# Another fixed order of the same 2689 steps in a chunked attention with a split-precision feed-forward layer

## The chip, the core and the metric

The kernel runs on one core of a Trainium2 chip. The metric is the device time of one execution in microseconds; less is better. The core has TensorE (PE, matmuls and transposes), VectorE (DVE), ScalarE (ACT), GpSimd (POOL) and SyncE (SP), which here issues every DMA transfer. Each engine works through its own list of instructions in order and waits for the others through semaphores.

## The reference

```python
def _attn_ref(q, k, v):                  # each (8, 8, 576, 64), float32
    q_c = q.reshape(B, H, nc, 64, D)     # chunks of 64 positions; k_c, v_c alike
    scores = scale * np.matmul(q_c, k_c.transpose(0, 1, 2, 4, 3))
    scores = scores - np.max(scores, axis=-1, keepdims=True)
    attn = np.exp(scores)
    attn = attn / (np.sum(attn, axis=-1, keepdims=True) + 1e-09)
    out = np.matmul(attn, v_c)
...
    x = attn_out.transpose(0, 2, 1, 3).reshape(B * S, H * D)   # (4608, 512)
    h = x @ w_in                          # w_in (512, 2048), float64
    g = h * (1.0 / (1.0 + np.exp(-1.702 * h)))
    return (g @ w_out).astype(np.float32) # w_out (2048, 512), float64
```

## The kernel before

The 4608 tokens are cut into 36 tiles of 128 and 9 blocks of 512. Attention makes x for a tile; the feed-forward part takes a block at a time through 16 slices of 128 hidden units. Each float32 product is made of three matmuls on a high and a low part (low x with high w, high x with high w, high x with low w), so x, g and the weights are all split in two. The first three blocks are computed plainly; the other six go in three pairs with seven instead of eight products for a 2 by 2 scheme of halves (`plan_two`), and the last pair's second matrix product too (`plan_o`).

All work is cut into steps. `plan.add(engine, cost, rank, fn, need, make, take, give)` names a step by its `make`: it needs other steps, takes buffers and gives them back. What order they are issued in is a string, `ORDER`, with the 2689 names in a row; `Plan.emit` runs through it and calls each step's function, so that every engine's list of instructions, SP's transfers among them, is the list of its steps in that order. The costs and ranks in `plan.add` decide nothing once the list is fixed. Two kinds of steps that the rows below show most:

- The first four token tiles (`plan_first`, u = 0 to 3), ahead of everything: load q and k (`q_u`, `k_u`) and v (`v_u`); transposes on PE (`tqp_u`, `tkp_u`, L453, tiles qkTp_u_0 and qkTp_u_1), copied out by ACT (`tq_u`, `tk_u`; tile 0's k by DVE); scores on PE (`s_u`, L474); row maximum and subtraction on DVE (`m_u`, `sm_u`, L480, L484); exponential on ACT (`ex_u`); sum and reciprocal on DVE (`z_u`, L491 to L494); normalisation on POOL (`n_u`, L497); transposes on PE (`ep_u`, L502), copied by ACT (`et_u`, L509); x on PE (`xp_u`, L518); x's high part on ACT (`xh_u`, L526), its low part on DVE (`xl_u`, L529). `xp_u` takes both buffers of the tag `att`, and `xl_u` gives them back, so one tile's x is read out before the next is made.
- The weights' 16 blocks (`plan_w`, j = 0 to 15): two loads of 512 KB of float64 words (`raw_j`, L335 and L339), scaling on ACT (`wsc_j`, L343), low words on ACT (`wlow_j`, L347), a shift on DVE (`wshift_j`, L352), a join on DVE (`wj_j`, L356), the high part on ACT (`wh_j`, L361), the low part on DVE (`w_j`, L366).

`h_g` are the first matmuls of slice g (L1446 to L1448; the first two slices in two halves of 256 tokens, L1457 to L1459), `gh_g` and `gl_g` the activation and its split, `o_g_t` the second matmuls (L1483 to L1485). `tp0_4`, `qk_...`, `v0_4` and the like belong to the attention of later tiles, which runs beside the feed-forward work.

Three steps hold matmuls of a constant whose result nobody reads: `warm` (7) and `fill_0`, `fill_1`, `fill_2`:

```python
    WARM = 7
    FILL = (5, 2, 5)
...
    def keep_warm(pool, tag, count):
        warm = pool.tile([P, P], F32, tag=tag, name="warm")
        for _ in range(count):
            nc.tensor.matmul(warm, ident, ident, start=True, stop=True)
```

## Time and profile before

| what | value |
|---|---|
| median of 3 runs (lowest, highest) | 823.83 us (823.46, 823.99) |
| the profiled execution | 823.62 us, of which its span 821.8 us and 1.8 us around it |
| busy: PE, DVE, ACT, POOL | 810.4, 582.6, 382.4, 89.8 us |
| HBM traffic | 130 MB, 158 GB/s over the span |
| mean granted TensorE clock | 0.996 of full speed |

The span runs from the first to the last instruction of one execution. Busy time is what instructions of an engine cover; matmuls are pipelined and their ends are modelled.

### The profile page before, as it was taken

The page shows a single profiled execution, that of the slowest core. Times are in us where ns is not written, and L with a number is a line of the kernel's source. Part 1 is how long each engine was busy: PE and PEld are TensorE (multiplying, and loading weights), DVE is VectorE, ACT ScalarE, POOL GpSimd, SP SyncE. Part 2 cuts the span into 40 slices and gives each one's busy share as a digit, 9 for nine tenths or more (in the row PEclk, how much of TensorE's full clock was granted, in tenths as well). Part 3 has the DMA queues.
Part 4 walks back from the last instruction along what each step waited for, and adds up shares of the span by engine and source line. Part 5 has one row for each costly group of instructions (what it writes and reads, how often), then busy time and mean ns, then how long its engine had stood idle before and what let it go on. Part 6 is the DMA issues. An engine that isn't in the chain of part 4 may idle for free.

```text
span 821.8 us, 15643 instructions
## 1 busy us (share of the span) xinstructions
PE 810.4 (99%) x6038; PEld 683.3 (83%) x6038; DVE 582.6 (71%) x861; ACT 382.4 (47%) x601; POOL 89.8 (11%) x82
## 2 busy tenths in 40 slices
PE   7999999999999999999999999999999999999998
PEld 6888888888888888778888887888788888889998
DVE  5688876445567788886697888776869444569952
ACT  5899734144354646323445352432555310447440
POOL 1000061000054650000001010100001000000000
PEclk9899999999999999999999999999999999999999
DMA  9999435741275768667575447766642047664523
GB/s 236 308 309 252 109 75 141 199 91 34 44 185 150 206 171 251 168 185 198 153 194 148 110 97 211 179 196 182 194 124 70 0 134 214 193 185 134 154 69 125
DMA packets 244010, 131.08 MB, mean 160 GB/s; under 512 B 187104, under 2 KB 211680, under 8 KB 243936
## 3 DMA queue, kind: packets, MB, share of 16 engines
q1 hardware_dynamic: 243936, 130.08, 58.7%
q8 instruction: 48, 0.79, 0.4%
q14 instruction: 26, 0.21, 0.1%
HBM read 97.52 MB, written 32.51 MB: 158 GB/s over the span
## 4 chain that ended last, share of the span: by engine, by line
PE 91%; DVE 4%; SPq 1%; ACT 1%; DMA 1%; issue 1%; DVEq 0%; ACTq 0%
PE po L1483 12%; PE po L1485 12%; PE po L1484 12%; PE hp L753 9%; PE hp L755 8%; PE hp L754 8%; PE hp L1446 5%; PE hp L1447 5%; PE hp L1448 5%; PE s L1226 2%; PE x L1300 2%; DVE eT L1275 2%; PE acc_X L1000 1%; PE acc_Z L1002 1%; PE acc_Z L1001 1%; PE acc_Z L1000 1%
## 5 line engine op out<-in xcount | busy, mean ns | idle before, releaser
L1483 PE MATMUL po<-w,g_l 128*128 128x512 f32 x448 | 176.5, 394 | 0.0
L1485 PE MATMUL po<-w,g_h 128*128 128x512 f32 x448 | 174.5, 390 | 0.0
L1484 PE MATMUL po<-w,g_h 128*128 128x512 f32 x448 | 174.5, 389 | 0.0
L1483 PEld LDWEIGHTS po<-w,g_l 128*128 128x128 f32 x448 | 84.1, 188 | 18.5 <-DVE g_l L1473 0.3
L1485 PEld LDWEIGHTS po<-w,g_h 128*128 128x128 f32 x448 | 84.1, 188 | 17.7
L1484 PEld LDWEIGHTS po<-w,g_h 128*128 128x128 f32 x448 | 84.1, 188 | 16.8
L1275 DVE STREAM_TRANSPOSE eT<-e 32x512 f32<-32x512 f32 x120 | 84.2, 702 | 6.7 <-POOL e L1256 4.8
L753 PE MATMUL hp<-w,w 128*128 128x512 f32 x224 | 87.6, 391 | 0.0
L755 PE MATMUL hp<-w,w 128*128 128x512 f32 x224 | 87.2, 389 | 0.0
L754 PE MATMUL hp<-w,w 128*128 128x512 f32 x224 | 87.2, 389 | 0.0
L1256 POOL TENSOR_TENSOR e<-e,r 128x1024 f32<-128x1024 f32 x16 | 31.5, 1969 | 451.9 <-DVE r L1253 390.3
L1446 PE MATMUL hp<-x_l,w 128*128 128x512 f32 x184 | 72.0, 391 | 0.0
L1447 PE MATMUL hp<-x_h,w 128*128 128x512 f32 x184 | 71.6, 389 | 0.0
L1448 PE MATMUL hp<-x_h,w 128*128 128x512 f32 x184 | 71.6, 389 | 0.0
L1473 DVE TENSOR_TENSOR g_l<-hp,g_h 128x512 fp32r<-128x512 f32 (+1 forms) x50 | 33.2, 666 | 42.3 <-ACT g_h L1468 42.0
L1467 ACT ACTIVATE hp<-hp 128x512 f32<-128x512 f32 (+1 forms) x50 | 28.4, 568 | 74.4 <-PE hp L1448 69.6
L768 ACT ACTIVATE d<-hp 128x512 f32<-128x512 f32 x24 | 14.2, 594 | 81.2 <-PE hp L755 80.5
L753 PEld LDWEIGHTS hp<-w,w 128*128 128x128 f32 x224 | 42.0, 188 | 10.1 <-DVE g L734 0.4
L755 PEld LDWEIGHTS hp<-w,w 128*128 128x128 f32 x224 | 42.1, 188 | 8.8
L754 PEld LDWEIGHTS hp<-w,w 128*128 128x128 f32 x224 | 42.1, 188 | 8.5
L753 PE MATMUL hp<-w,pieces 128*128 128x512 f32 x112 | 44.0, 393 | 1.4 <-DVE d L734 0.7
L754 PE MATMUL hp<-w,pieces 128*128 128x512 f32 x112 | 43.6, 389 | 0.0
(237 smaller groups left out, 1592.3 us busy)
## 6 DMA issues: line engine op xcount, KB each, us to landing
w<-seven SPq DMA_DIRECT2D x112, 256.0 KB, 3.2
pieces<-seven SPq DMA_DIRECT2D x56, 256.0 KB, 3.1
seven<-w SPq DMA_DIRECT2D x24, 512.0 KB, 3.7
raw<-in_moe_w_in_dram SPq DMA_DIRECT2D x16, 512.0 KB, 6.5
raw<-in_moe_w_out_dram SPq DMA_DIRECT2D x16, 512.0 KB, 6.4
four<-four_w SPq DMA_DIRECT2D x32, 256.0 KB, 3.3
raw<-in_q_dram SPq DMA_DIRECT2D x208, 32.0 KB, 2.2
raw<-in_k_dram SPq DMA_DIRECT2D x208, 32.0 KB, 2.4
```

The lines of the kernel that those rows point to most:

```text
L753: nc.tensor.matmul(hp, w[:, 0, c], xl[:, c], start=c == 0, stop=False)
L754: nc.tensor.matmul(hp, w[:, 0, c], xh[:, c], start=False, stop=False)
L755: nc.tensor.matmul(hp, w[:, 1, c], xh[:, c], start=False, stop=c == 1)
L1256: nc.gpsimd.tensor_tensor(st["e"], st["e"], bc(st["r"]), op=ALU.mult)
L1275: nc.vector.transpose(st["et"][po : po + 32, :, 32 * a : 32 * a + 32], st["e"][pi : pi + 32, :, 32 * b : 32 * b + 32],)
L1446: nc.tensor.matmul(hp, wh, xl, start=cc == 0, stop=False)
L1447: nc.tensor.matmul(hp, wh, xh, start=False, stop=False)
L1448: nc.tensor.matmul(hp, wl, xh, start=False, stop=cc == NCC - 1)
L1473: nc.vector.tensor_tensor(gl[:, c], hp, gh[:, c].bitcast(F32), op=ALU.subtract)
L1483: nc.tensor.matmul(po, gl[:, c], w[:, 0, :], start=first, stop=False)
L1484: nc.tensor.matmul(po, gh[:, c], w[:, 0, :], start=False, stop=False)
L1485: nc.tensor.matmul(po, gh[:, c], w[:, 1, :], start=False, stop=last)
```

## The change

`ORDER` holds the same names in another order. The new list begins

```diff
-    "xa_0 xa_1 q_0 k_0 warm k_1 q_2 k_2 tqp_0 tkp_0 tq_0 q_1 fill_0 tk_0 raw_0 s_0 tqp_2 m_0 k_3 tkp_2 tq_2 sm_0 "
...
+    "xa_0 xa_1 k_1 q_1 warm q_0 k_3 k_0 tqp_1 q_3 tkp_1 tq_1 tqp_0 tk_1 q_2 s_1 tq_0 k_2 tkp_3 m_1 tkp_0 tk_3 sm_1 "
+    "raw_0 tk_0 ex_1 tqp_3 z_1 s_0 tq_3 v_1 v_0 s_3 n_1 m_0 sm_0 tkp_2 raw_1 m_3 ex_0 tqp_2 sm_3 tk_2 ep_1 tq_2 z_0 "
...
+    LOW_DVE = ()
...
-            nc.scalar.activation(li, lu, AF.Copy, scale=2.0**-29)
+            if j in LOW_DVE:
+                nc.vector.tensor_scalar(li, lu, 2.0**-29, None, op0=ALU.mult)
+            else:
+                nc.scalar.activation(li, lu, AF.Copy, scale=2.0**-29)
...
-        plan.add(ACT, 0.95, rank, scale, need=[e("raw")], make=e("wsc"))
-        plan.add(ACT, 0.95, rank, low, need=[e("wsc")], make=e("wlow"))
+        plan.add(ACT, 1.03, rank, scale, need=[e("raw")], make=e("wsc"))
+        if j in LOW_DVE:
+            plan.add(DVE, 0.6, rank, low, port=True, need=[e("raw")], make=e("wlow"))
+        else:
+            plan.add(ACT, 1.03, rank, low, need=[e("wsc")], make=e("wlow"))
...
-        plan.add(PE, 0.58, rank, lambda: t_pe(0), need=[ev("q")], make=ev("tqp"), take=["hp"])
+        plan.add(PE, 0.58, rank, lambda: t_pe(0), need=[ev("q"), "warm"], make=ev("tqp"), take=["hp"])
```

`LOW_DVE` is empty, so every block's low words stay on ACT; the new costs decide nothing in a fixed list; and `need` gains `"warm"` for the first tiles' transposes and the three fills, which stand behind `warm` in both lists. What changes in the program is the order alone. The lines of the kernel after it are up to seven higher.

**PE, around the x of the first tiles.** The rows are the thirteenth to the last one ahead of the feed-forward work and its first matmul. In eTp_u and x_u the first number is the tile u; warm is a group of dummies; hp_0_0 is the first feed-forward tile. Before:

```order
L502 MATMUL eTp_0_237<-ident_73,first_b_0_158 128x128 x4
L453 MATMUL qkTp_3_0_245<-ident_73,first_a_3_150 128x128 x4
L474 MATMUL s_3_260<-first_a_3_150 64x64 x16
L502 MATMUL eTp_1_291<-ident_73,first_b_1_225 128x128 x4
L518 MATMUL x_1_302<-first_b_1_225 64x64 x16
L502 MATMUL eTp_2_323<-ident_73,first_b_2_220 128x128 x4
L1560 MATMUL warm_333<-ident_73 128x128 x5
L518 MATMUL x_0_346<-first_b_0_158 64x64 x16
L502 MATMUL eTp_3_364<-ident_73,first_b_3_296 128x128 x4
L518 MATMUL x_2_376<-first_b_2_220 64x64 x16
L1457 MATMUL hp_0_0_393<-x_l_0_85,w_0_284 128x256
```

After:

```order
L509 MATMUL eTp_1_234<-ident_73,first_b_1_156 128x128 x4
L481 MATMUL s_2_246<-first_a_2_122 64x64 x16
L509 MATMUL eTp_0_278<-ident_73,first_b_0_192 128x128 x4
L525 MATMUL x_1_284<-first_b_1_156 64x64 x16
L1567 MATMUL warm_307<-ident_73 128x128 x5
L1567 MATMUL warm_320<-ident_73 128x128 x5
L525 MATMUL x_0_335<-first_b_0_192 64x64 x16
L509 MATMUL eTp_2_355<-ident_73,first_b_2_276 128x128 x4
L1567 MATMUL warm_364<-ident_73 128x128 x2
L509 MATMUL eTp_3_370<-ident_73,first_b_3_231 128x128 x4
L525 MATMUL x_2_380<-first_b_2_276 64x64 x16
L1464 MATMUL hp_0_0_399<-x_l_0_85,w_0_368 128x256
```

Before, five dummies (`fill_0`, not in these rows) stand ahead of the first scores, five (`fill_2`) between tile 2's transposes and tile 0's x, and two (`fill_1`) behind the twelve matmuls of hp_0_0. After, `fill_0` and `fill_2` stand together between the x of tile 1 and of tile 0, and `fill_1` behind tile 2's transposes; none stands ahead of the scores or behind hp_0_0.

**DVE, over the same stretch.** m, z and first_b belong to the first tiles, wtmp and w to the weight block in their first number, x_l is the low part of x. Before:

```order
L480 TENSOR_REDUCE m_3_286<-s_3_260 128x8
L484 TENSOR_TENSOR first_b_3_296<-s_3_260,m_3_286 128x512
L366 TENSOR_TENSOR w_0_284<-wtmp_0_234,w_0_284 128x2x512
L491 TENSOR_REDUCE z_3_328<-first_b_3_296 128x8
L492 TENSOR_SCALAR z_3_328<-z_3_328 128x8
L494 RECIPROCAL r_3_331<-z_3_328 128x8
L529 TENSOR_TENSOR x_l_0_85<-x_1_302,x_h_0_84 128x4x128
L352 TENSOR_SCALAR wtmp_1_344<-raw_1_173 128x1024
L529 TENSOR_TENSOR x_l_0_85<-x_0_346,x_h_0_84 128x4x128
L356 ISA wtmp_1_344<-raw_1_173,wtmp_1_344 128x2048
L529 TENSOR_TENSOR x_l_0_85<-x_2_376,x_h_0_84 128x4x128
L366 TENSOR_TENSOR w_1_410<-wtmp_1_344,w_1_410 128x2x512
```

After:

```order
L356 TENSOR_SCALAR wtmp_0_301<-raw_0_158 128x1024
L498 TENSOR_REDUCE z_2_314<-first_b_2_276 128x8
L499 TENSOR_SCALAR z_2_314<-z_2_314 128x8
L501 RECIPROCAL r_2_317<-z_2_314 128x8
L360 ISA wtmp_0_301<-raw_0_158,wtmp_0_301 128x2048
L536 TENSOR_TENSOR x_l_0_85<-x_1_284,x_h_0_84 128x4x128
L356 TENSOR_SCALAR wtmp_1_353<-raw_1_220 128x1024
L360 ISA wtmp_1_353<-raw_1_220,wtmp_1_353 128x2048
L536 TENSOR_TENSOR x_l_0_85<-x_0_335,x_h_0_84 128x4x128
L370 TENSOR_TENSOR w_0_368<-wtmp_0_301,w_0_368 128x2x512
L370 TENSOR_TENSOR w_1_378<-wtmp_1_353,w_1_378 128x2x512
L536 TENSOR_TENSOR x_l_0_85<-x_2_380,x_h_0_84 128x4x128
```

The low part of weight block 0 moved from ahead of tile 3's sum to behind tile 0's low part of x, and follows directly on the join of block 1 and that x; the low part of block 1 comes right behind it, where before it stood behind tile 2's x.

**SP, the loads from weight block 6 or 12 to block 7.** raw_j from in_moe_w_in and in_moe_w_out is weight block j; raw_6 from in_q and in_k is the q and k of token tiles 6 and 7; rows_4 and v_4 are for tiles 4 and 5. Before:

```order
L335 DMA raw_4_407<-in_moe_w_in_dram 128x4x128
L339 DMA raw_4_407<-in_moe_w_out_dram 128x512
L415 DMA rows_4_369<-in_q_dram 128x8x64
L415 DMA rows_4_369<-in_k_dram 128x8x64
L335 DMA raw_6_474<-in_moe_w_in_dram 128x4x128
L339 DMA raw_6_474<-in_moe_w_out_dram 128x512
L335 DMA raw_5_518<-in_moe_w_in_dram 128x4x128
L339 DMA raw_5_518<-in_moe_w_out_dram 128x512
L335 DMA raw_7_525<-in_moe_w_in_dram 128x4x128
L339 DMA raw_7_525<-in_moe_w_out_dram 128x512
```

After:

```order
L336 DMA raw_12_545<-in_moe_w_in_dram 128x4x128
L340 DMA raw_12_545<-in_moe_w_out_dram 128x512
L336 DMA raw_6_597<-in_moe_w_in_dram 128x4x128
L340 DMA raw_6_597<-in_moe_w_out_dram 128x512
L1174 DMA raw_6_532<-in_k_dram 32x8x32 x4
L336 DMA raw_8_636<-in_moe_w_in_dram 128x4x128
L340 DMA raw_8_636<-in_moe_w_out_dram 128x512
L1189 DMA v_4_499<-in_v_dram 64x8x64 x2
L1174 DMA raw_6_532<-in_q_dram 32x8x32 x4
L336 DMA raw_7_691<-in_moe_w_in_dram 128x4x128
L340 DMA raw_7_691<-in_moe_w_out_dram 128x512
```

Block 7 came directly behind blocks 4, 6 and 5. Now blocks 12, 6 and 8, two groups of q and k and two loads of v stand between block 5 and block 7.

## Rows read from the trace of the kernel before

**Rows 1.** From the page of the whole execution: busy us (and share of the span) of each engine, and the row of the attention's stream transposes on VectorE (busy us, mean ns of one, idle time before them).

```profile
PE 810.4 (99%) x6038; PEld 683.3 (83%) x6038; DVE 582.6 (71%) x861; ACT 382.4 (47%) x601; POOL 89.8 (11%) x82
...
L1275 DVE STREAM_TRANSPOSE eT<-e 32x512 f32<-32x512 f32 x120 | 84.2, 702 | 6.7 <-POOL e L1256 4.8
```

**Rows 2.** Busy time by stretches of the span. After the stretch and its length: busy us of PE, PEld, DVE, ACT and POOL with the number of instructions, the granted TensorE clock, the DMA share and GB/s.

```profile
0.00:5.92 5.92, 4.56 (x21) 4.53 (x22) 0.00 (x0) 1.60 (x2) 0.70 (x6) 1.00 0.81 156
5.92:19.58 13.66, 9.90 (x172) 8.52 (x171) 10.00 (x19) 8.68 (x15) 2.08 (x2) 1.00 1.15 277
19.58:26.40 6.82, 5.97 (x83) 5.11 (x82) 5.07 (x8) 4.93 (x7) 2.08 (x2) 0.50 1.07 293
320.00:370.00 50.00, 48.99 (x333) 39.94 (x332) 42.62 (x65) 17.34 (x28) 1.90 (x1) 1.00 0.69 184
```

**Rows 3.** Time line of PE in the first 32 us: start, us, line, operation, count (one matmul or transpose on fp32 data shows as two records, so five dummies are x10), and in brackets the idle time before and what ended it.

```profile
1.36 3.35 PE L1560 MATMUL warm<-ident 128*128 128x128 f32 x14 [1.36 <-POOL ident masks.py:199]
4.50 1.73 PE L453 MATMUL qkTp<-ident,first_a 128*128 128x128 f32 x8
6.25 1.38 PE L1560 MATMUL warm<-ident 128*128 128x128 f32 x10
7.56 1.15 PE L474 MATMUL s<-first_a 64*64 64x64 f32 x32
...
22.98 2.34 PE L1560 MATMUL warm<-ident 128*128 128x128 f32 x10
25.25 1.13 PE L518 MATMUL x<-first_b 64*64 64x64 f32 x32
...
28.50 0.39 PE L1457 MATMUL hp<-x_l,w 128*128 128x256 f32 x1
...
30.04 0.61 PE L1560 MATMUL warm<-ident 128*128 128x128 f32 x4
30.58 0.69 PE L518 MATMUL x<-first_b 64*64 64x64 f32 x32
...
31.43 0.28 PE L1458 MATMUL hp<-x_h,w 128*128 128x256 f32 x1
```

**Rows 4.** The chain of work that ended last, in order of time: start, us, what.

```profile
30.21 1.22 DVE w L366
```

**Rows 5.** Time line of DVE in the first 32 us, columns as in rows 3.

```profile
8.76 0.69 DVE L480 TENSOR_REDUCE m<-s 128x8 f32<-128x512 f32 x1 [1.79 <-PE s L474]
...
10.97 0.69 DVE L491 TENSOR_REDUCE z<-first_b 128x8 f32<-128x512 f32 x1 [0.80 <-ACT first_b L487]
...
12.26 0.69 DVE L480 TENSOR_REDUCE m<-s 128x8 f32<-128x512 f32 x1 [0.16 <-PE s L474]
...
14.91 0.69 DVE L352 TENSOR_SCALAR wtmp<-raw 128x1024 int32<-128x1024 int32 x1
...
27.09 0.69 DVE L529 TENSOR_TENSOR x_l<-x,x_h 128x512 fp32r<-128x512 f32 x1 [2.26 <-ACT x_h L526]
```

**Rows 6.** Groups of instructions by line and form in the first 61 us: count, busy us, mean ns of one, idle time before them.

```profile
L343 ACT ACTIVATE raw<-raw 128x1024 f32<-128x1024 f32 x9 | 10.0, 1138 | 1.8 <-DMA raw<-in_moe_w_out_dram 1.8
...
L366 DVE TENSOR_TENSOR w<-wtmp,w 128x1024 fp32r<-128x1024 f32 x7 | 8.5, 1222 | 3.3 <-ACT w L361 3.3
L356 DVE CUSTOM_DVE_ANT_0 wtmp<-raw,wtmp 128x2048 uint16<-128x2048 uint16 x7 | 8.5, 1220 | 1.2 <-ACT raw L347 1.2
...
L361 ACT ACTIVATE w<-wtmp 128x1024 fp32r<-128x1024 f32 x7 | 7.3, 1053 | 0.0
...
L352 DVE TENSOR_SCALAR wtmp<-raw 128x1024 int32<-128x1024 int32 x8 | 5.9, 746 | 1.4 <-ACT raw L343 1.4
```

**Rows 7.** The first loads: the first row of the time line of SP's DMA queue; the first use of weight block 0 on ACT; the spread of time from issue to landing of q and k of the first four tiles; GB/s in 40 equal slices of the first 62 us.

```profile
0.73 0.45 SPq L415 DMA_DIRECT2D first_a<-in_q_dram  x1
...
13.56 1.10 ACT L343 ACTIVATE raw<-raw 128x1024 f32<-128x1024 f32 x1 [1.65 <-DMA raw<-in_moe_w_out_dram]
...
DMA to landing us min/median/max: 3.2/5.0/7.0
...
GB/s 0 164 253 217 216 219 357 338 235 222 406 298 158 323 368 260 286 379 276 158 333 371 259 294 279 348 390 342 383 246 219 323 267 314 369 381 293 284 347 181
```

**Rows 8.** What the DMA engines moved in the first 62 us, and in 36 to 62 us.

```profile
DMA packets 29027, 17.60 MB, mean 284 GB/s; under 512 B 21248, under 2 KB 27485, under 8 KB 29021
...
DMA packets 9068, 8.08 MB, mean 311 GB/s; under 512 B 4551, under 2 KB 8169, under 8 KB 9065
```

**Rows 9.** Time line of PE at three later places, columns as in rows 3.

```profile
36.27 0.40 PE L1485 MATMUL po<-w,g_h 128*128 128x512 f32 x1
36.74 0.39 PE L1457 MATMUL hp<-x_l,w 128*128 128x256 f32 x1
...
60.47 0.39 PE L1447 MATMUL hp<-x_h,w 128*128 128x512 f32 x1
60.70 0.39 PE L1448 MATMUL hp<-x_h,w 128*128 128x512 f32 x1
61.11 0.50 PE L1446 MATMUL hp<-x_l,w 128*128 128x512 f32 x1
...
333.54 0.39 PE L1485 MATMUL po<-w,g_h 128*128 128x512 f32 x1
334.43 0.50 PE L753 MATMUL hp<-w,pieces 128*128 128x512 f32 x1 [0.50 <-DVE g L734]
```

More of the change, by code (lines that the diff above doesn't have):

```diff
@@ L536, in plan_first @@
         plan.add(DMA, (1, 1.05, 1024), u - 101.5, load_v, make=ev("v"), take=[slot(1)])
-        plan.add(PE, 0.58, rank, lambda: t_pe(0), need=[ev("q")], make=ev("tqp"), take=["hp"])
-        plan.add(PE, 0.58, rank, lambda: t_pe(1), need=[ev("k")], make=ev("tkp"), take=["hp"])
+        plan.add(PE, 0.58, rank, lambda: t_pe(0), need=[ev("q"), "warm"], make=ev("tqp"), take=["hp"])
+        plan.add(PE, 0.58, rank, lambda: t_pe(1), need=[ev("k"), "warm"], make=ev("tkp"), take=["hp"])
         plan.add(ACT, 0.5, rank, t_q, need=[ev("tqp")], make=ev("tq"), give=["hp"])
@@ L1568, in tile_chunk_attention_ffn @@
         plan.add(
-            PE, 0.23 * n, -1000, lambda n=n: keep_warm(ps_h, "hp", n), make=f"fill_{i}", take=["hp"], give=["hp"],
+            PE, 0.23 * n, -1000, lambda n=n: keep_warm(ps_h, "hp", n), need=["warm"], make=f"fill_{i}", take=["hp"], give=["hp"],
         )
```

341 rows, old and new, of the table ORDER are left out of this document.

## Prediction

> **What bounds the kernel now.** I read the engines' busy times first [rows 1]: TensorE (PE) is busy in 810.4 of 821.8 us. The change issues the same steps in another order, so only PE's waits and its clock can change the time. The table by stretches [rows 2] says where most waits are: 6.0 us before 26.40, and of what is left 1.0 in 320 to 370. The Trainium skill ("Trainium Kernel Development and Optimization", Reading a trace) calls matmul busy time a bad metric, since matmuls are pipelined; the trace agrees: a matmul is listed with 0.39 us where the next one starts 0.23 later [rows 9], so a short wait hides under a full busy share, and I take waits from starts instead.
>
> The clock comes next. The stretch 19.58 to 26.40 was granted 0.50, 1.2 of 2.4 GHz, and ten dummy matmuls there took 2.34 us, where ten at 1.00 took 1.38 [rows 2, 3]. The first stretch is printed with 1.00, but its 14 warm-up matmuls took 3.35 us, 0.24 each, which is the pace of the 0.50 stretch. I read it as the lower level up to 5.92.
>
> Then the head. The first feed-forward matmul starts at 28.50, and PE has real work without a break only from the second matmul of the next tile, at 31.43 [rows 3]. The chain of waits says what it waited for: the low part of weight block 1 on VectorE (DVE), 30.21 to 31.43, which reads what ACT has made of the same block [rows 4]. Whatever is to be won is mostly in front of this point.
>
> **The change part by part.** The new list starts the attention with tile 1, loads all q and k before the first weight, and puts all three groups of dummy matmuls in front of the first feed-forward matmul. I follow its chain.
>
> *Start.* The first load lands 3.2 us after its issue at 0.73, so at 3.9; at 217 GB/s a 256 KB load takes 1.2 us, so the second lands at 5.1 [rows 7]. The new list's first transposes (q of tile 1) read the second load. Before, tile 0's q was transposed from 4.50 on and only its k waited for the second load; both were through at 6.23, the scores started 1.3 us later, after a copy on ACT and one on DVE, took 1.15, and DVE's first maximum began at 8.76 [rows 3, 5]. Now both transposes come after 5.1 and are through some 0.3 us later, but without a group of dummies between them and the scores: the maximum begins at about 8.8. That holds if the clock rises at 5.92 again. But PE now has nothing from the end of warm-up (4.7) to 5.1, where before it went straight on. If the clock rises only with a later stretch, transposes and scores take up to twice as long, and the maximum starts near 10.0 (about 1.2 later). I take the later value, because the pause is real and no row shows a pause there that did no harm; 8.8 is the other end.
>
> *DVE's list.* From this maximum to block 1's low part it holds: four pairs of maximum and subtraction (0.66 from start to start: four in 12.26 to 14.91), four sums with reciprocal (1.13: 10.97 to 12.10), one copy (as long as a maximum, 0.69), two shifts (0.75), two joins and two low parts (1.22 each), two low parts of x (0.69) [rows 5, 6]. That is 5.3 + 4.5 + 0.7 + 1.5 + 4.9 + 1.4 = 18.3 us; with 0.3 for small holes I take 18.6, where before DVE idled 2.26 us for tile 0's x [rows 5]. Block 1's low part ends at 10.0 + 18.6 = 28.6 (27.4 with the early clock). Before it is 31.43, but there tile 3's x matmuls had already run (30.58 to 31.21, 0.63 us), and in the new list they still stand behind. So the comparison is 31.43 - 0.63 = 30.80 to 28.6: **2.2 us** (3.4 with the early clock). The 0.54 us of dummy matmuls at 30.04 are in this sum: they now run in front, where PE waits for tile 1's x to be read out.
>
> *Loads.* Block 0 of the weights moves two loads back. Before it was there at 13.56, after six loads [rows 7]; behind eight it is there at about 16.0, its scaling (1.14, [rows 6]) and the low word, as long, end by 18.3, and DVE wants them for the join at about 20: hidden. On ACT the same wait holds up tile 2's exponential and tile 0's transposed weights behind it, by about 1 us that these have in hand. Block 1 lands near 22; ACT's scaling then ends at 23, about when DVE comes to its shift (22.3 with the early clock, 23.5 with the late one). So in the early case the loads take some of the gain back. GpSimd's four normalisations change order with the sums and wait for nothing else.
>
> *Waits further on.* Before, PE lost 0.24 us at 36.5 (start to start 0.47 instead of 0.23) and 0.18 at 60.9 [rows 9]; these belong to the old order of the weights' passes, and I count 0.5 with the small ones beside them as gone, since the weights' passes are the ones that were moved most. Against that I count 0.3 for a transpose behind tile 3's low part of x and for block 6 (below). The waits in 320 to 370 come where a product's drain stands on DVE behind other drains and stream transposes of 0.70 us each [rows 1]: 333.54 to 334.43 is 0.66 more than the usual 0.23 [rows 9]. The new list permutes these pieces too; it has as many of them, so I leave their sum unchanged, with 1 us to either side (the stretch's waits gone, or as much again).
>
> Sum: 2.2 + 0.5 - 0.3 = 2.4 us. The profiled execution took 823.62 (span 821.8 and 1.8 around it), 0.2 below the median: 821.2 against it, and **821.4** against the median 823.83.
>
> **The rivals.** A difference below 0.2% (1.65 us) can't be told from no change here.
>
> *The clock rises as early as before.* Then 3.6 by the same sum, less some for block 1's landing: 820.2 to 820.6. The only evidence against it is the pause of half a microsecond.
>
> *The clock falls again before the feed-forward matmuls.* It fell at 19.58 after a stretch with PE busy in 9.90 of 13.66 us [rows 2]. In the new list the first group of dummies has left the front and stands beside another between the x of tiles 1 and 0, where PE waits for DVE to read tile 1's x. At half clock an x group takes 0.44 us longer (1.13 for 0.69, [rows 3]); two of them and two groups of transposes lie in the stretch, about 1.6 in all, of which I let 1.1 reach the path: gain 1.3, 822.5. If the low stretch falls on feed-forward work, 6.8 us of it cost 3.4, and the result is 824.8 at worst. The Trainium skill ("TensorE: Matmul & The Clock Gate", Part 1) says the throttled clock is the default and activity releases it; the trace agrees, with 0.50 granted just where PE had waited most. By that rule moving dummies out of the front speaks against the change.
>
> *The weights' loads become the wait.* Block 7's load stands behind blocks 12, 6 and 8 now, and ACT must scale it before it writes block 6's high part. 15.6 MB are ahead of or in it (12 first-tile loads and 4 row loads of 0.26, ten blocks of 1.05, 0.9 of small ones). With 17.6 MB by 62.0 and 311 GB/s in the last 26 us [rows 8] it lands at 55.5; with 5% less pace and 2 us for the gaps at the small loads, at 58.6. Then 1.14 + 1.05 + 1.22 us [rows 6] give block 6 at 58.9 to 62.0. Before, PE comes to it at 61.1; in the new list some 2.6 us more of other work stands in front (six more 512-column matmuls, and tile pair 4's transposes and x), and that starts 2.2 earlier: about 61.5. So it is free or costs 0.5. Landing at 60, it costs 1.9: 823.3, no change to be seen.
>
> *Slower: the drains in the middle.* The DVE is packed in 320 to 370 (42.6 of 50 us, [rows 2]). Where one more transpose pair falls ahead of a drain, PE stops for some 0.6 us as at 334. Seven such places more than now (there are 24 groups of products) eat the 2.4 and 1.65 beyond: it decides there; eight give 823.83 - 2.4 + 4.8 = 826.2. Against it: DVE idles over a tenth of even that stretch, and the new list has no more work for it.
>
> **How the numbers follow.** Sum as worked out, 820.4 to 822.2: 0.50. Early clock: 0.14. Clock falls again: 0.15 (nearly all of it within 0.2%). Weights' loads or another small wait that gives the gain back: 0.14. Slower through the drains: 0.07. Faster takes the first two and a little of the third, 0.66; within 0.2%, 0.27; slower 0.07. The range runs from 819.8 (early clock, and half of the middle waits gone) to 823.3 (loads).
>
> **What would show it.** Right: the first feed-forward matmul near 27 and its second tile without a wait at about 28.6; DVE from about 10 to 28 without a hole over 1 us; the dummies all ahead of 25; no wait at 36 or 61. The first maximum at 8.8 or 10.0 says which clock it was. Wrong: a granted clock of 0.50 after 26, a DMA wait on ACT's scaling at 55 to 62, more than 1.5 us of PE waits in 320 to 370, or a start of the chain at 10.0 followed by holes on DVE where a first-tile x or a weight block is late.

## The result: slower by 0.7%, though the head gained

| | before | after |
|---|---|---|
| median (lowest to highest) | 823.59 us of 7 runs (823.46 to 824.28) | 828.69 us of 7 runs (826.23 to 831.48) |
| profiled execution, its span | 823.62, 821.8 us | 828.05, 826.3 us |

The ratio is 1.0068 (95% interval 1.0054 to 1.0082): 5.1 us slower, where 2.4 us faster was predicted. The runs also lie further apart than those of before: 5.2 us against 0.8.

The page's engine row and the table of stretches after the change, with the columns of [rows 1, 2]; the stretches 28.50 to 110 and 370 to 500 are new here:

```profile
PE 810.8 (98%) x6038; PEld 679.2 (82%) x6038; DVE 586.2 (71%) x861; ACT 384.2 (46%) x601; POOL 90.9 (11%) x82
```

```profile
0.00:5.92 5.92, 4.14 (x21) 3.85 (x22) 0.00 (x0) 1.35 (x2) 0.70 (x6) 1.00 0.76 156
5.92:19.58 13.66, 10.77 (x205) 9.06 (x203) 9.91 (x20) 8.78 (x15) 3.13 (x3) 1.00 1.16 270
19.58:26.40 6.82, 3.92 (x77) 3.43 (x80) 5.68 (x9) 6.79 (x10) 1.85 (x1) 1.00 1.08 297
28.50:45.00 16.50, 16.50 (x187) 14.24 (x186) 12.66 (x16) 16.11 (x23) 0.00 (x0) 1.00 1.00 275
45.00:62.00 17.00, 16.07 (x74) 12.88 (x73) 12.06 (x14) 14.06 (x18) 1.91 (x1) 1.00 0.94 260
62.00:110.00 48.00, 47.50 (x324) 37.83 (x323) 41.47 (x47) 38.86 (x46) 4.46 (x3) 1.00 0.74 207
320.00:370.00 50.00, 49.80 (x338) 40.91 (x338) 42.52 (x65) 16.42 (x26) 1.91 (x1) 1.00 0.66 168
370.00:420.00 50.00, 49.32 (x333) 39.68 (x332) 33.20 (x53) 20.39 (x35) 1.91 (x1) 1.00 0.74 198
420.00:500.00 80.00, 78.05 (x573) 62.09 (x572) 70.23 (x106) 38.40 (x66) 3.81 (x2) 1.00 0.47 118
```

PE's busy time is the same, and its clock is full in all these stretches behind the warm-up (its 14 matmuls took 3.36 us, 0.24 each, as before): the stretch from 19.58, at 0.50 before [rows 2], is granted 1.00. What is longer is PE's idle time: 0.93 us in 45 to 62, 0.50 in 62 to 110, 0.68 in 370 to 420 and 1.95 in 420 to 500. Only 320 to 370, the one stretch for which the prediction looked at waits in the middle, got better: 0.20 us idle where it was 1.0.

Busy time hides short waits, so I also took, for every two neighbouring matmuls, the distance of their starts less the usual distance for such a pair, and added these up (us, the two profiled executions; how the usual distance of a rare pair is taken moves a stretch by up to some 0.3 us, and more ahead of 45, so only differences are used there):

| | before | after | difference |
|---|---|---|---|
| start of the first feed-forward matmul | 28.50 | 26.71 | -1.79 |
| waits to 45 | -0.63 | -0.85 | -0.22 |
| 45 to 110 (weights still arriving) | 1.97 | 3.96 | +1.99 |
| 110 to 320 | 7.61 | 7.64 | +0.03 |
| 320 to 370 | 2.68 | 1.55 | -1.13 |
| 370 to 500 | 3.64 | 9.05 | +5.41 |
| 500 to the end | 5.15 | 5.18 | +0.03 |

The differences add up to 4.3 us; the last matmul starts 4.4 later (818.41, 822.85). From 420 to 500 the new list costs the same in every profiled execution that has it unchanged there (6.3 to 6.4 us in after, e4, f3 and h2, 2.6 before); 370 to 420 varies (1.2 to 2.7, 1.1 before), and so do the other two stretches with loads: in runs whose lists are the same there as after's, 45 to 110 comes to 1.3 us (e3) and 1.7 (j1) as well as to some 4 (after, j3), and behind 500 to anything from 5.2 (after, e4) to 8.5 (e3, h2). That is as much as the scatter of the runs.

**The head.** PE's time line after the change, to be held against [rows 3]:

```profile
1.36 3.36 PE L1567 MATMUL warm<-ident 128*128 128x128 f32 x14 [1.36 <-POOL ident masks.py:199]
5.14 1.11 PE L460 MATMUL qkTp<-ident,first_a 128*128 128x128 f32 x8 [0.42 <-DMA first_a<-in_q_dram]
...
22.52 0.69 PE L525 MATMUL x<-first_b 64*64 64x64 f32 x32 [1.50 <-DVE x_l L536]
23.64 0.61 PE L1567 MATMUL warm<-ident 128*128 128x128 f32 x4
26.08 0.69 PE L525 MATMUL x<-first_b 64*64 64x64 f32 x32 [1.40 <-ACT first_b L516]
26.71 0.38 PE L1464 MATMUL hp<-x_l,w 128*128 128x256 f32 x1
```

DVE's, to be held against [rows 5]: its first maximum, and all its waits over 0.3 us from 13 us to block 1's low part (the second of the two in the last row).

```profile
8.68 0.69 DVE L487 TENSOR_REDUCE m<-s 128x8 f32<-128x512 f32 x1 [8.68 <-PE s L481]
...
23.11 0.69 DVE L356 TENSOR_SCALAR wtmp<-raw 128x1024 int32<-128x1024 int32 x1 [0.64 <-ACT raw L344]
24.16 1.23 DVE L360 CUSTOM_DVE_ANT_0 wtmp<-raw,wtmp 128x2048 uint16<-128x2048 uint16 x1 [0.35 <-ACT raw L351]
...
25.90 2.35 DVE L370 TENSOR_TENSOR w<-wtmp,w 128x1024 fp32r<-128x1024 f32 x2
```

The maximum starts at 8.68: the early clock, with 8 transposes in 1.11 us. Block 1's low part ends at 28.25, against 30.80 by the prediction's reckoning for before. Its early case said 27.4; 1.0 us went into waiting for ACT's scaling and low words of that block, the landing that the prediction had named.

**The weights.** ACT's time line: the scalings of blocks 8 and 7, which wait for their loads (the trace writes the q load as the releaser, whose tile is called raw too). Then PE's.

```profile
55.16 1.14 ACT L344 ACTIVATE raw<-raw 128x1024 f32<-128x1024 f32 x1 [2.01 <-DMA raw<-in_q_dram]
...
60.73 1.17 ACT L344 ACTIVATE raw<-raw 128x1024 f32<-128x1024 f32 x1 [0.43 <-DMA raw<-in_q_dram]
```

```profile
57.30 0.50 PE L1453 MATMUL hp<-x_l,w 128*128 128x512 f32 x1 [0.41 <-ACT w L365]
...
58.55 0.50 PE L1455 MATMUL hp<-x_h,w 128*128 128x512 f32 x1 [0.53 <-DVE w L370]
```

Block 8 lands at 55.00 and is wanted by ACT at 53.1; behind its scaling in ACT's list stands the high part of block 5 (56.20), and PE waits for block 5. Block 7 landed at 60.65; the prediction had 55.5 to 58.6. Held against ACT's list, the new order has little in hand: before, every load of the blocks 2 to 15 had landed 0.8 us or more before ACT came to its scaling; after, seven of the fourteen (2, 3, 6, 8, 7, 11, 15) had landed less than 0.3 us before. Two of those, 8 and 7, made ACT wait more than 0.1 us.

**The middle.** The longest wait of the whole run, on PE:

```profile
483.04 0.39 PE L1492 MATMUL po<-w,g_h 128*128 128x512 f32 x1
485.09 0.50 PE L1490 MATMUL po<-w,g_l 128*128 128x512 f32 x1 [1.67 <-DVE g_l L811]
```

and what DVE and GpSimd do there after the change (two time lines):

```profile
480.72 1.22 DVE L1257 TENSOR_REDUCE z<-e 128x16 f32<-128x1024 f32 x1
...
482.19 0.25 DVE L1260 RECIPROCAL r<-z 128x16 f32<-128x16 f32 x1
482.77 2.27 DVE L811 TENSOR_TENSOR g_l<-g,g_h 128x512 fp32r<-128x512 f32 x1 [0.33 <-ACT g_h L807]
```

```profile
482.58 1.90 POOL L1263 TENSOR_TENSOR e<-e,r 128x1024 f32<-128x1024 f32 x1 [36.08 <-DVE r L1260]
```

and before the change:

```profile
481.56 0.26 DVE L1253 RECIPROCAL r<-z 128x16 f32<-128x16 f32 x1
481.73 0.63 DVE L804 TENSOR_TENSOR g_l<-g,g_h 128x512 fp32r<-128x512 f32 x1
```

```profile
481.96 2.17 POOL L1256 TENSOR_TENSOR e<-e,r 128x1024 f32<-128x1024 f32 x1 [35.67 <-DVE r L1253]
```

The low part of g (`gl_74`) takes 2.27 us instead of 0.69. It starts 0.19 us after GpSimd's normalisation `n_28` (482.58 to 484.48) and ends at 485.04, 0.56 after it: held for as long as the normalisation runs, and then done. Both its inputs, g and g_h, lie in SBUF; the low part `g_l<-hp,g_h` of another slice, whose hp lies in PSUM, took its usual 0.69 us at 171.30, under a normalisation that ran from 170.64 to 172.55. Before, `gl_75` stood there; it started 0.23 us ahead of the normalisation and took 0.63, and the normalisation took 2.17 instead of 1.90. The same happens at 445 (`gl_78`, 2.07). The Trainium skill ("SBUF — State Buffer", "SBUF: two separate sides" and "Who interferes with whom") says that a DVE instruction with two inputs in SBUF contends with a GpSimd instruction that reads SBUF, whoever starts first keeps the shared ports for its whole length, and the other is blocked. These rows agree, with 1.4 to 1.6 us of holding. That is a rule that spoke against this change, and the prediction did not weigh it.

The trace of before showed the same in a place where it cost PE nothing. DVE and GpSimd:

```profile
619.13 1.12 DVE L804 TENSOR_TENSOR g_l<-g,g_h 128x512 fp32r<-128x512 f32 x1
```

```profile
617.54 2.16 POOL L1256 TENSOR_TENSOR e<-e,r 128x1024 f32<-128x1024 f32 x1 [33.01 <-DVE r L1253]
```

So a row of 1.12 us among rows of 0.69 could have been found, and asked about, ahead of the prediction.

### The profile page after: what moved, and what is told of

It is laid out like the page before. It is cut to its first block, busy times and chain, and to the rows that moved or that the text cites. A ratio compares the mean times of both kernels' runs of the same rounds, so it can differ in the third digit from the quotient of the medians.

```text
span 826.3 us, 15637 instructions
## 1 busy us (share of the span) xinstructions
PE 810.8 (98%) x6038; PEld 679.2 (82%) x6038; DVE 586.2 (71%) x861; ACT 384.2 (46%) x601; POOL 90.9 (11%) x82
## 4 chain that ended last, share of the span: by engine, by line
PE 80%; DMA 7%; SPq 7%; DVE 4%; issue 1%; ACT 1%; DVEq 0%; ACTq 0%
PE po L1490 11%; PE po L1492 10%; PE po L1491 10%; PE hp L760 8%; PE hp L761 8%; PE hp L762 8%; DMA raw<-in_moe_w_out_dram 5%; PE hp L1453 4%; PE hp L1455 4%; PE hp L1454 4%; SPq L336 2%; PE s L1233 2%; SPq L422 2%; PE x L1307 2%; SPq L1174 1%
## 5 line engine op out<-in xcount | busy, mean ns | idle before, releaser
L760 PE MATMUL hp<-w,pieces 128*128 128x512 f32 x112 | 44.0, 393 | 0.2 <-DVE g L741 0.2
L762 PE MATMUL hp<-w,pieces 128*128 128x512 f32 x112 | 43.6, 389 | 0.0
L761 PE MATMUL hp<-w,pieces 128*128 128x512 f32 x112 | 43.6, 389 | 0.0
```

Source lines behind the costliest of these rows:

```text
L760: nc.tensor.matmul(hp, w[:, 0, c], xl[:, c], start=c == 0, stop=False)
L761: nc.tensor.matmul(hp, w[:, 0, c], xh[:, c], start=False, stop=False)
L762: nc.tensor.matmul(hp, w[:, 1, c], xh[:, c], start=False, stop=c == 1)
```

## The experiments

In the diffs, a line of names is a piece of `ORDER`. A list spliced from two has the first one up to the step named and then what is left in the second one's order. Times are medians with the ratio to runs of the kernel before on the same chip (822.99 to 823.72) and its interval.

### Which part of the list costs

```diff
-ORDER: the new list
+e4: the old list up to gh_47 (312 us), then the new one
+e1: the new list up to l4x_0_1 (312 us), then the old one
+f1: the new list up to o_30_3 (200 us), then the old one
+h1: the new list up to raw_4 (31 us), then the old one
```

> The list before up to the first seven-product group, the new list from there on. Theory M: the middle's 4.3 us without the head's gain, less the 0.5 by which the new list waits less behind 500: 827.4 (826 to 829), and runs that scatter by 2 us or more. Rival W: 823.6, since the loads are as before. Rival P: 823.6 to 825, since nothing has moved when the middle begins.

Measured 828.61 (1.0067; 1.0055 to 1.0079): all of the loss with the old head, as theory M said. PE has the waits of after, at 409, 446, 455, 483 (1.83 by starts; its row is below) and 543. At 409 it is a product's load that came last here (1.05 by starts), where in after it was a sum on DVE (0.54).

```profile
484.98 0.50 PE L1488 MATMUL po<-w,g_l 128*128 128x512 f32 x1 [1.67 <-DVE g_l L809]
```

> The new list up to the first seven-product group (P1_0_0, at about 312 us), the list before from there on. In the new kernel's trace PE's waits stand 4.3 us above those of before between 320 and 500 us and 1.7 above between 45 and 110, against a head that starts the feed-forward work 2.3 us earlier (dummies counted). Theory M (the middle costs: drains and low parts held on DVE behind 320 us): 823.6 - 2.3 + 1.7 = 823.0, and runs that lie within 1 us of each other as those of before do. Rival W (the weights' loads at 45 to 62 us set the loss, and the middle only follows): no better than 827. Rival P (any shift of the head lets steps in the middle collide that did not before, whatever the list): 825 or more.

Measured 827.33 (1.0051; 1.0038 to 1.0063). A miss, and a bad cut: at the joint, where the two lists are out of step, PE waits 1.40 at 312.6 and 1.12 at 327, which neither list has. So I cut again where there is slack.

> The new list up to the scores of tile pair 14 (about 200 us, where both lists have issued the same steps but two), the list before from there on. It has no joint inside the seven-product groups, where the first such splice stood 2.5 us at its joint. Theory M (the middle of the new list costs, its first 200 us gain): before less 1.2 to 2.3 for the head, plus 0 to 2.6 for late weight blocks: between 1.5 below and 1 above the kernel before, and no new wait behind 320 us. Rival P (a shift of the whole by 1 to 2 us is enough for collisions in the middle): 2 us or more above before, with new waits in 320 to 600.

Measured 823.91 (1.0002; 0.9993 to 1.0011): no change. The first feed-forward matmul is at 26.75, so the gain is there, and the waits of 0.63, 0.68 and 0.76 at slices 5, 9 and 14 take it back. In the middle it has the old waits (0.67 at 334 and at 365) and none of the new ones.

> The new list up to block 4's load (about 31 us), the list before from there on: the new attention head with the old order of all weight blocks from 4 on. In the trace of before ACT scales block 6 4.6 us, block 7 1.6 us and block 8 4.5 us after its landing, so a head that is 1.2 to 2.4 us earlier takes up to 0.8 us of a wait at block 7 and none at the others. Theory L (the head's gain is real, and in the other splices the weights' loads took it back): 0.8 to 2.0 us below the kernel before, no new wait over 0.5 us from 45 on. Rival P: 1 us or more above.

Measured 824.29 (1.0012; 1.0003 to 1.0021), not 0.8 to 2.0 below the kernel before. The first matmul is at 26.73, but the joint costs: the matmuls behind tile 3's x wait 1.44 us for that x to be read out, and ACT waits 1.46 for the load of block 3, with a slice's g behind it in its list (PE 0.57 at 36.67). So this splice doesn't show what the head is worth by itself. What f1 and e4 give adds up: nothing from the first 200 us, the whole 5 us from behind 312.

### The weights' loads

```diff
-tk1_4 raw_12 s_4 ... wj_4 raw_8 gh_2 ... wlow_5 raw_7 o_3_0     (new)
+e2: the new list up to raw_12, then the old one
+f2: as e2, with raw_12 moved to behind wj_7
+f3: tk1_4 s_4 ... wj_4 raw_8 gh_2 ... wlow_5 raw_7 raw_12 o_3_0
+h2: tk1_4 s_4 ... wj_4 raw_8 raw_12 gh_2 ... wlow_5 raw_7 o_3_0
+j2: f1 with raw_6 raw_8 raw_7 in a row and all of block 12's steps behind block 9's
```

> The new list up to the scores of tile pair 4 (s_4, about 37 us), the list before from there on, so the weights' loads from block 6 on stand as before except block 12, which was already issued. Theory M: the head's whole 2.3 us and nothing of the later waits, 821.3. Rival W: about 821.5 as well if loads set the loss, 823 if block 12's early load delays the others by its 3 us. Rival P: 824 or more, with new waits of over 0.5 us somewhere in 320 to 500.

> The new list up to the scores of tile pair 4 (about 37 us) without block 12's load, then the list before. The first such splice had block 12's 1 MB ahead of block 6's: ACT, in order, waited for block 6, the activation of slice 2 stood behind it, and PE waited 4.18 us and lost its clock for some us. Theory L (that one load was all of it): no wait over 0.5 us between 45 and 62, and 1.2 to 2.4 us below the kernel before. Rival P: 1 us or more above before.

Both were misses. e2 took 830.43 (1.0091; 1.0077 to 1.0105): with block 12's load in front, ACT waits 3.02 us at 49.95 for block 6 and PE 4.18, and PE is then at half clock until 59. f2, without it, took 825.77 (1.0038; 1.0025 to 1.0051), 2.4 us above before where 1.2 to 2.4 below was expected, with waits of 1.09 and 0.61 left; so that one load was not all of it.

> The new list with block 12's load moved from ahead of block 6 to behind block 7, so blocks 6, 8 and 7 come about 3 us earlier. Theory W (weights that land late cost the new list 0 to 2.6 us between 45 and 110 us, by how the loads fall): the waits at the slices 5 and 6 go, 827.5 against the 828.7 of the new kernel, its lowest runs unchanged near 826. Rival: no change, 828.7, since those waits were gone in half of the profiled executions anyway.

Measured 831.45 (1.0095; 1.0077 to 1.0113): a miss through my own edit. I moved the load and left the scaling where it stood; ACT idles 3.97 us at 60.52 for block 12, with the g of slice 4 behind it, and PE waits 2.79. It shows the mechanism all the same: ACT's list, not the need of a block, decides who waits.

> The new list with block 12's load behind block 8's, ahead of block 7's: ACT scales 8 ahead of 12, so both orders now agree, and only blocks 6 and 8 come some 4 us earlier, 12 later; all the other loads stay. Theory W: in the new kernel's trace ACT idled 2.01 us for block 8, which landed at 55.00, and the high part of block 5 stood behind it; that wait goes, PE's waits between 45 and 62 fall from 1.6 to about 0.4, 828.7 to about 827.7, and the low runs near 826 stay. Rival: block 12 then holds ACT as it did when it was loaded behind block 7, and the time is 829 or more.

Measured 828.07 (1.0038; 1.0024 to 1.0052). Locally as expected (block 8 lands at 50.33 instead of 55.00, PE's waits in 45 to 62 fall from 1.27 to 0.55), in the total (0.6 below after) within the scatter.

> The list that is new up to about 200 us and old after, with weight blocks 6, 8 and 7 loaded directly behind each other in the order in which ScalarE wants them, and block 12 (load, scaling, low words, shift, join and parts) moved back behind block 9's. If the head's gain of 2.3 us is lost only because blocks 8 and 7 land late behind block 12, the waits of 1.3 us at 57 to 63 are gone, ScalarE has no wait for a load over 0.5 us between 45 and 65, and the time is 823.9 - 1.3 = 822.6, or 822.2 with the restarts (821.4 to 823.2). The rival, that the transfers as a whole are the limit (share of the DMA engines over 1 until 62), brings the same waits back at later blocks (9, 10, 12 at 70 to 85): 823.6 to 824.4.

Measured 826.28 (1.0040; 1.0028 to 1.0052). The waits at 45 to 62 are gone, 0.23 left, but behind block 9's scaling ACT now waits 5.37 us for block 12, and PE 3.36:

```profile
75.14 1.12 ACT L342 ACTIVATE raw<-raw 128x1024 f32<-128x1024 f32 x1 [5.37 <-DMA raw<-in_moe_w_out_dram]
```

The rival's mechanism, at more than its price. In 60 to 78 us the two loads of a block land 6.1 and 6.7 us (medians) after issue, with twelve loads of 32 KB for q and k among them and the DMA engines busy for 86%; that these small loads are the reason is not shown. In f3 and j2 moving a load made the block that was moved the late one, and in i2 below it made block 7 late. In h2, and in i1 below, it did not: their waits in 45 to 110 are 2.6 and 2.0, near before's.

### GpSimd's normalisation and DVE's low parts

```diff
 e3 (new list)
-z_28 o_73_3 gh_74 ... gl_74 n_28 tq1_30
+o_73_3 gh_74 ... gl_74 z_28 n_28 tq1_30          (and z_26 behind gl_78)
 g1 (old list)
-o_73_0 t3x_1_1 o_73_3 z_28 h4x_1_1
+o_73_0 z_28 t3x_1_1 o_73_3 h4x_1_1
 j1
+            if u in (26, 28):
+                return
             nc.gpsimd.tensor_tensor(st["e"], st["e"], bc(st["r"]), op=ALU.mult)
 j3
+            for a in range(0, NG, NG // 2):
+                sl = slice(a, a + NG // 2)
+                nc.gpsimd.tensor_tensor(st["e"][:, sl], st["e"][:, sl], rb[:, sl], op=ALU.mult)
```

> The new list, with two steps moved: the row sums z_26 and z_28 (and so the start of the normalisations n_26 and n_28 on GpSimd) go behind the low parts gl_78 and gl_74 on DVE. In the new kernel's trace these two low parts took 2.07 and 2.27 us instead of 0.69, each begun 0.2 to 0.4 us after a normalisation had started on GpSimd and ended 0.5 us after it, and PE stood 0.33 and 1.83 us. Theory S (a low part with both operands in SBUF waits out a running normalisation): both take 0.69, PE's two waits shrink to 0.4 or less, 828.7 - 1.9 = 826.8 (to 826.2), and the spread of runs becomes smaller. Rival D (DVE is just full there, and the low parts come late anyway): 828.0 to 828.7, the waits move to the next drain.

Measured 827.77 (1.0049; 1.0033 to 1.0064), between the two theories and within the scatter of after. `gl_74` and `gl_78` take 0.69, and the wait at 483 falls to 0.25. But the hold has moved to the next low part. The time lines of DVE and GpSimd:

```profile
483.10 1.25 DVE L1215 STREAM_TRANSPOSE qkT<-raw 128x1024 f32<-128x1024 f32 x1
484.27 1.38 DVE L809 TENSOR_TENSOR g_l<-g,g_h 128x512 fp32r<-128x512 f32 x1
```

```profile
483.19 1.91 POOL L1261 TENSOR_TENSOR e<-e,r 128x1024 f32<-128x1024 f32 x1 [36.36 <-DVE r L1258]
```

`gl_75` was held until the normalisation ended at 485.10, and PE waited 1.33 at 484. The stream transpose ahead of it, with one input, began 0.09 us before the same normalisation and ran beside it at its usual 1.24. So that execution lost most of it again 1 us later, and more at a product's load:

```profile
563.02 0.39 PE L1490 MATMUL po<-w,g_h 128*128 128x512 f32 x1
565.32 0.47 PE L758 MATMUL hp<-w,w 128*128 128x512 f32 x1 [1.91 <-DMA w<-seven]
...
566.49 0.63 PE L759 MATMUL hp<-w,w 128*128 128x512 f32 x1
566.92 0.63 PE L760 MATMUL hp<-w,w 128*128 128x512 f32 x1
```

After that wait the matmuls start 0.43 apart instead of 0.23, the pace of the half clock. Where this load stands in SP's queue, before and after:

```profile
549.81 0.37 SPq L740 DMA_DIRECT2D w<-seven  x1
```

```profile
559.06 0.45 SPq L747 DMA_DIRECT2D w<-seven  x1
```

Before, it landed at 554.1, 5.7 us ahead of its product. In the new list it lands at 564.0 to 565.6 (in j1, which is 5.7 us ahead there, at 558.7), and PE waits 0 (after), 0.35 (j1), 0.54 (j3), 0.71 (e4), 1.19 (f3), 2.07 (e3) or 2.41 (h2) for it. This is one source of the scatter.

> The list before with one step moved by one place: the row sum z_28 on DVE goes ahead of t3x_1_1, so it ends some 0.7 us earlier, and with it starts the normalisation n_28 on GpSimd. In the trace of before the low part gl_75 started right at the end of the sum, 0.23 us ahead of the normalisation, and took 0.63 us; the part's high half is ready 0.1 us before that. Theory S (a low part with both operands in SBUF that finds a normalisation running waits it out): n_28 now starts near 481.3 (ends 483.2 to 483.4), gl_75 starts at about 481.7, ends after it, and takes 1.7 to 2.2 us; PE's next second matmul of slice 75 waits up to 0.5 us, and the time rises by 0 to 0.5. Rival D (low parts are late only because DVE is full): gl_75 takes 0.6 to 0.7 us as before and nothing changes.

Measured 824.16 (1.0015; 1.0006 to 1.0023), 0.8 us slower with one place moved. DVE and GpSimd:

```profile
483.38 1.08 DVE L809 TENSOR_TENSOR g_l<-g,g_h 128x512 fp32r<-128x512 f32 x1 [1.22 <-ACT g_h L805]
```

```profile
481.76 2.15 POOL L1261 TENSOR_TENSOR e<-e,r 128x1024 f32<-128x1024 f32 x1 [35.35 <-DVE r L1258]
```

`gl_75` comes 1.65 us later than before (ACT makes its high part later, since the transform ahead of it moved too), falls under the normalisation, and PE waits 1.0 at 483.29. Of that delay only 0.39 us are holding (1.08 for 0.69, where 1.7 to 2.2 was expected), so g1 shows that the hold can be put into the old list, but not that it is what made this run slower.

> The new list with the GpSimd normalisation of two token pairs (u = 26 and 28) left out, so their outputs are not normalised; all other instructions and the order stay. If it is GpSimd's normalisation that holds VectorE's low parts gl_78 (2.07 us at 445) and gl_74 (2.27 us at 483), both take 0.69 us here, TensorE's waits of 0.33 at 446.5 and 1.83 at 483 are gone with a restart of 0.11 each, and the time is 828.7 - 2.4 = 826.3 us (825.3 to 827.4; the wait for a late product load near 563 still varies by some 2 us from run to run). The rival, that these low parts are late for another reason (they stand too far down VectorE's list), leaves them near 2 us and the time at 828.0 to 829.0.

Measured 826.59 (1.0040; 1.0023 to 1.0058), 2.1 us less than after where 2.4 was forecast; but the runs of both scatter so widely that the two intervals overlap, and it is the trace that shows the size. DVE and PE where after waited 1.67:

```profile
478.66 0.69 DVE L811 TENSOR_TENSOR g_l<-g,g_h 128x512 fp32r<-128x512 f32 x1 [0.35 <-ACT g_h L807]
```

```profile
478.93 0.39 PE L1494 MATMUL po<-w,g_h 128*128 128x512 f32 x1
479.41 0.50 PE L1492 MATMUL po<-w,g_l 128*128 128x512 f32 x1
```

It is the holding and not the place: the same instruction in the same place of DVE's list takes 0.69, and PE loses 0.25 instead of 1.83. The sum of waits in 420 to 500 falls from 6.33 to 3.97. The profiled execution took 822.77, a little less than the old list's 823.22 beside it: in it the loads were also in time (no wait over 0.14 between 45 and 110). Its eight runs go from 822.8 to 829.7, so the scatter is not the work of these two normalisations.

> The new list with each pair's normalisation on GpSimd as two instructions of half the size (about 1.0 us each in place of 1.9). If VectorE is held until the running GpSimd instruction ends and then gets in, the holds of gl_78 and gl_74 end up to 0.95 us earlier: the wait at 483 falls from 1.83 to about 0.9 and that at 446.5 goes, 827.5 us (826.4 to 828.5). If the second half starts without letting VectorE in, nothing changes: 828.7.

Measured 826.93 (1.0052; 1.0034 to 1.0071): inside the range, but not clear of after's 1.0054 to 1.0082. The row is clearer: `gl_74` takes 1.41 and PE waits 0.97 at 481 (0.9 expected). The low part ends 0.55 us after the half that runs (482.00) and not after the second (481.96 to 483.45), so cutting the normalisation shortens the hold.

### Mending several places

```diff
 i1 (new list)
-tk1_4 raw_12 s_4 ... o_11_2 wj_15 gh_12 ... gl_74 n_28 tq1_30 ... P3_1_4 ld2_1_5 ld1_1_5 ld3_1_5
+wj_4 raw_8 raw_12 ... gl_12 wj_15 ... gl_75 z_28 n_28 ... ld0_1_5 ld1_1_5 d1_1_4 ... P7_1_4 ld2_1_5
 i2 (f1's list)
+the same moves of raw_12 and wj_15, and tq1_6 from behind h_8 to behind wj_9
```

> The new list with four small moves, one for each place that the traces name: block 12's load behind block 8's; block 15's join wj_15 behind the low part gl_12 on DVE (PE stood 0.55 to 0.76 us at h0_14, whose bank gl_12 frees); the loads ld1_1_5 and ld2_1_5 some 5 us earlier in SP's list (they landed 0.6 to 2.4 us after PE wanted the product P2_1_5 at 563 us); the row sum z_28 behind both low parts gl_74 and gl_75. Theory A (the loss is a sum of places where a step comes just too late, each with its own price): the waits at 57, 106, 483 and 563 us go, 0.6 + 0.6 + 1.8 + 1.5 on average, so 828.7 - 4.5 = 824.2, and the spread shrinks to 2 us. Rival F (DVE and the queue are full, so a step that is moved makes the next one late): 827 or more, with new waits of the same size next to the old places.

Measured 827.59 (1.0056; 1.0037 to 1.0076): the waits named are gone (57, 106, 563; 0.25 left at 483), and the gain is not, as rival F said. The normalisation (483.29 to 485.45) now holds a difference of two halves of x, with `gl_76` behind it (DVE's time line):

```profile
483.72 2.27 DVE L596 TENSOR_TENSOR xs<-xs,g 128x512 f32<-128x512 f32 x1
```

PE waits 1.96 at 485, and then comes a stretch at half clock (the table of stretches, columns as above):

```profile
484.00:488.00 4.00, 2.20 (x10) 1.44 (x9) 3.87 (x4) 2.10 (x5) 1.44 (x1) 1.00 0.41 65
488.00:492.00 4.00, 4.00 (x12) 3.04 (x11) 3.92 (x7) 2.87 (x4) 0.00 (x0) 0.57 0.00 0
492.00:496.00 4.00, 4.00 (x19) 3.32 (x18) 3.49 (x6) 1.74 (x4) 0.00 (x0) 1.00 0.00 0
```

> The new list up to 200 us and the list before from there on (823.9 when it ran, level with before), with three moves: block 12's load behind block 8's, wj_15 behind gl_12, and the transposed q and k of tile 6 (tq1_6) behind block 9's join on DVE, since PE stood 0.63, 0.76 and 0.68 us at those places. Theory A: the three waits go, 1.5 to 2.3 us, so 822.0, some 1.4 below the kernel before. Rival F: 823 to 825, with waits at the next weight block or at the scores s_6.

Measured 823.61 (1.0009; 0.9999 to 1.0020), rival F again. The named waits are gone, and in the profiled execution PE waits 1.39 and 0.70 between 62 and 66 for the blocks' parts; ACT has waited 0.87 for the load of block 12 and 1.93 for that of block 7. No kernel here is measurably faster than the one before.

## Why the prediction was wrong

**What bounds the kernel: right.** PE is as busy as before and only its waits changed. But the search for waits stopped at the stretches where the old list has them. That says where the old order is bad; where the new one is bad it can't say.

**Start and DVE's list: right in mechanism, 0.7 to 0.9 us off in size.** 2.2 us was predicted with the late clock, 3.4 with the early one. The profile of after has the early clock and 30.80 - 28.25 = 2.55, 0.85 less than its case, since DVE waited 1.0 for block 1 where 0.3 for small holes was counted. Both clocks occur: in e3 the first transposes and the first feed-forward matmul (PE's time line) were

```profile
5.40 2.91 PE L458 MATMUL qkTp<-ident,first_a 128*128 128x128 f32 x12 [0.68 <-DMA first_a<-in_q_dram]
...
27.79 0.38 PE L1462 MATMUL hp<-x_l,w 128*128 128x256 f32 x1
```

1.08 us behind after's, where the two cases were put 1.2 apart; block 1's low part ended at 29.33 there, a gain of 1.47 for the 2.2. That 2.55 lies near the 2.2 of the sum is luck: the sum took the late clock, this execution had the early one, and the missing wait makes up for it. The dummies all ran ahead of 25, DVE had no hole over 1 us, the waits at 36 and 61 are gone, and the clock did not fall before the feed-forward matmuls.

**Waits further on, the weights: mis-sized.** 0.3 us was counted; 45 to 110 costs 2.0 more than before in the profiled execution, and nothing more in those of e3 and j1, whose loads of block 8 and 7 were earlier (in e3 53.51 and 58.92). The bound was worked out for block 7 alone (55.5 to 58.6; landed 60.65). Not looked at: block 8, whose scaling stands in ACT's list ahead of block 5's high part, and the joins and low parts of the last blocks (0.67 at 106). The step that failed here is to ask of one load when it lands, instead of walking down ACT's list and asking it of each. ACT's wait of 2.01 ahead of 55.16 is also one of the signs of being wrong that the prediction named. f1 shows the outcome: new up to 200 us, no gain.

**Waits further on, the middle: the step that failed most.** "It has as many of them, so I leave their sum unchanged, with 1 us to either side" was a count of pieces. 320 to 370 came out 1.1 us shorter, but 370 to 500 is +5.4, and e4 shows that the new list behind 312 us alone makes the kernel as slow as it is. Of it, j1's trace shows 2.4 to be two normalisations that hold two low parts. The drain behind a sum at 409 is a case that the prediction had priced right (0.54, priced 0.6); PE and DVE there:

```profile
409.77 0.47 PE L760 MATMUL hp<-w,w 128*128 128x512 f32 x1 [0.38 <-DVE z L1257]
```

```profile
408.41 1.22 DVE L1257 TENSOR_REDUCE z<-e 128x16 f32<-128x1024 f32 x1 [0.93 <-ACT e L1253]
```

The rest, some 2.5 us, is six waits of 0.14 to 0.46 (the longest, at 381, for the load of a product) and many below, and I found no single cause for them; it stays open. DVE is busy 70.23 of 80 us in 420 to 500, where it was 67.69 before (69.87 in j1, where the two holds are gone), so it may be that a low part that comes late by a little has nothing to catch up in; no run shows it. What a run pays beyond that depends on when its loads land: this part (57, 62, 563) differs between executions by some 2.7 us in 45 to 110 and 3.3 behind 500, half-clock stretches included, and was only seen in profiles, not separated by a run of its own.

**The rivals.** The slower side was foreseen as DVE's drains in the middle, at 0.07, with seven places of 0.6 us as the point of decision. The side and the engine are right, the stretch and the largest mechanism found (an instruction stretched by another engine, not a queue of drains) are not. The chance was too small for a term that nothing bounded: 180 us of a repacked DVE list were covered by one sentence.

## What to carry to other kernels

A fixed list that is free of long waits is tight in places that its own profile doesn't show, so when the steps are put in another order, walk each in-order engine's new list through the whole run (each load against the first step that wants it, each drain against what stands ahead of it), and widen the range for every stretch not walked. Keep DVE instructions with two SBUF inputs that feed PE out from under a GpSimd instruction, by running them just ahead of it or by cutting it into shorter ones (both seen here in single rows; neither made a kernel measurably faster). A step's duration depends on what runs beside it, and a load's on the other loads, so durations traced under one order are not those of another.

## What the runs showed of the hardware that I had not expected

DVE's low part of 0.69 us takes 1.08 to 2.27 us when it starts while GpSimd's 1.9 us normalisation runs, and ends about 0.55 us after it; a stream transpose with one input is not held (1.25 at 285.11 in after, begun 0.66 us into a GpSimd instruction of 1.91). A shift with one input, at 49.75 in after, was: 2.14 instead of 0.69 us, with a normalisation from 49.43 to 51.34. After an idle time of PE of 1.80 us in i1 and 1.91 in e3 the next matmuls started 0.43 instead of 0.23 us apart for some 4 us (granted clock 0.57 in i1's 488 to 492), while the 1.67 us at 483 in after, but also 2.25 at 565.70 in h2 and 2.62 at 63.51 in f3, were followed by full speed (granted 1.00). So a wait can cost nearly as much again behind it, and its length alone does not say whether it will.
